# q of batches 0 and 1 loaded and transposed in the layout of k: 2 KB pieces, 64 transposes of a quarter of the array each

## The chip, the cores and the metric

The kernel runs on one core of a Trainium2 chip. The metric is the device time of one execution in microseconds; lower is better. A profiled execution also gives a *span*, from the first to the last recorded event, which is about 1.8 us shorter than the time.

## The reference, cut to what matters

A linear attention (softmax of q along its 64 features, softmax of k along its 576 tokens, no softmax of their product) is followed by a two-layer network with an exact gelu:

```python
# q, k, v: 8 batches x 8 heads x 576 tokens x 64, float32
q_s = softmax(q, axis=-1)
k_s = softmax(k, axis=2)
kv  = einsum('bhsd,bhse->bhde', k_s, v)
x   = einsum('bhsd,bhde->bhse', q_s, kv)     # -> 4608 x 512
h   = x @ w_in                               # 512 x 2048
out = gelu(h) @ w_out                        # 2048 x 512
```

The two products of the network are nearly all of the work. They run in bfloat16 as matmuls of 128x128 weights with 512 columns.

## The kernel before: the parts that matter

Tokens are worked off in nine groups of 512. Eight groups hold 512 of a batch's 576 tokens each; the 64 that are left of every batch make up the ninth. For the attention product of a group, q must lie with its 64 features along the partitions. Batches 0 and 1, which are needed early, are transposed by TensorE; the others by a DMA. Before, a partition held four consecutive tokens of every head, so one piece of memory was 4 x 64 x 4 B = 1 KB:

```python
def load_main(b, name, t, parts=1):          # q of batches 0 and 1, in two transfers
    ...
    src = t[b, :, 0:M, :].rearrange("h (p j) d -> p h (j d)", j=J)      # M = 512, J = 4
    ...

def exp_q(b, parts=1):
    ...
    if parts == 1:      # four instructions of 512 columns, each touching heads of both halves
        sets = [(slice(i, None, 4), slice(u, None, 4)) for i, u in ((0, 0), (1, 1), (2, 3), (3, 2))]
    else:               # six instructions; the first three complete heads 0 to 3
        sets = []
        for h in (0, 4):
            sets += [(slice(h + i, h + i + n), slice(h + u, h + u + n))
                     for i, u, n in ((0, 0, 2), (2, 3, 1), (3, 2, 1))]
    for i, u in sets:
        nc.scalar.activation(out=dst[:, i], in_=src[:, u], func=AF.Exp)

def tp_mm(b, half):                          # 8 transposes of 128x128: two heads x 64 features
    ...
    for i in range(2):
        hp = 2 * half + i
        for j in range(J):
            nc.tensor.transpose(ps[:, j, i, :],
                st[b]["eq"][:, j, 2 * hp:2 * hp + 2, :].rearrange("p h d -> p (h d)"), identity)
```

A word on names, for the profiles below. L355 is line 355 of that kernel's file, so the same operation has another number in each kernel. `e` and `ek` are exp of q and of k, `qsum` the sums by which q is normalised, `qT` the transposed q, `kvc` the normalised product of k and v, `ps` and `tp` banks of the accumulator memory, `xT` the result of the attention product and the input of the first big product, `g` the gelu's output, `wi_bf` and `wo_bf` the two weights. A *tile* of the first big product is 128 of its 2048 columns and takes four matmuls of 0.216 us.

The normalising of q is done in halves (four heads each), the first half on GpSimd and the second on VectorE. Batch 2 is the first whose q is transposed by a DMA. That transfer sits in the second product of batch 1, and the attention product of batch 2 (`x_all(2)`) follows later in the same stage:

```python
exp_q(2, parts=2)
exp_k(2)
exp_k(3)
exp_q(3)
table(AF.Gelu)
y_phase(1, {
    (0, 15): [lambda: norm_q(2, 0, 2)],
    (1, 1): [lambda: norm_q(2, 1, 2, nc.vector)],
    (1, 14): [lambda: kv_step(2)],
    (1, 15): [lambda: xbar_step(2)],          # q of batch 2 transposed by a DMA
    (2, 2): [lambda: cast_v_all(3), lambda: load(4)],
    (3, 5): [lambda: x_all(2), lambda: kv_step(3)],
})
```

The softmax here doesn't subtract the row's maximum and nothing guards it: scores larger than these inputs give would overflow.

## Time and profile before

| | kernel before |
|---|---|
| time, three executions ahead of the prediction | 279.63 to 279.91 us |
| span of the profile | 278.0 us |
| TensorE busy | 270.0 us |
| first matmul of the first big product | 14.32 us |
| second big product of batch 0 begins | 28.15 us |
| attention product of batch 2 begins | 70.98 us |

The last rows are stations on TensorE's road. TensorE is the bound, so a change matters by what it does to the time at which TensorE comes past such a station. What TensorE itself waited for is a short list. Its columns are: who waits, for whom, us in total, how often, and the longest; "issue" is time in which the engine waited for nothing that the profile shows.

```profile
PE ps L475 <- DVE zeros L500: 1.5, 1, 1.5
PE ps L355 <- issue: 1.1, 7, 0.2
PE ps L294 <- DVE kvc L218: 0.6, 1, 0.6
PE kv L199 <- ACT v_aug L160: 0.2, 1, 0.2
```

The first is the warming at the very start. The other two named waits are short and lie in batch 0's start. No wait on a transfer appears: in particular none on the transposed q of batch 2.

### The profile page before, as it was taken

The page shows a single profiled execution, that of the slowest core. Times are in us where ns is not written, and L with a number is a line of the kernel's source. Part 1 is how long each engine was busy: PE and PEld are TensorE (multiplying, and loading weights), DVE is VectorE, ACT ScalarE, POOL GpSimd, SP SyncE. Part 2 cuts the span into 40 slices and gives each one's busy share as a digit, 9 for nine tenths or more (in the row PEclk, how much of TensorE's full clock was granted, in tenths as well). Part 3 has the DMA queues.
Part 4 walks back from the last instruction along what each step waited for, and adds up shares of the span by engine and source line. Part 5 has one row for each costly group of instructions (what it writes and reads, how often), then busy time and mean ns, then how long its engine had stood idle before and what let it go on. Part 6 is the DMA issues. An engine that isn't in the chain of part 4 may idle for free.

```text
span 278.0 us, 4534 instructions
## 1 busy us (share of the span) xinstructions
PE 270.0 (97%) x1891; PEld 126.5 (46%) x1919; DVE 100.7 (36%) x153; ACT 158.0 (57%) x247; POOL 32.8 (12%) x26
## 2 busy tenths in 40 slices
PE   7899999999999999999999999999999999999995
PEld 3444454444444444444444444444444444444443
DVE  2876574319743540093008400651015200130012
ACT  4867675789377816791569246943683363136400
POOL 1520051002020220014000500050005000000000
PEclk9999999999999999999999999999999999999999
DMA  7999999963993139702981199017502500220033
GB/s 253 398 386 429 397 402 407 398 257 103 287 348 61 66 79 295 283 38 86 267 329 40 42 247 383 38 51 190 115 0 75 151 2 0 75 78 0 0 78 77
DMA packets 44980, 50.10 MB, mean 180 GB/s; under 512 B 20384, under 2 KB 29856, under 8 KB 44704
## 3 DMA queue, kind: packets, MB, share of 16 engines
q1 hardware_dynamic: 44560, 49.39, 53.5%
q10 hardware_dynamic: 400, 0.43, 0.6%
q8 instruction: 15, 0.25, 0.3%
q14 instruction: 5, 0.04, 0.0%
HBM read 36.70 MB, written 9.44 MB: 166 GB/s over the span
## 4 chain that ended last, share of the span: by engine, by line
PE 94%; DMA 2%; issue 1%; ACT 1%; SPq 1%; DVE 0%
PE ps L327 44%; PE ps L355 43%; DMA f<-in_k_dram 2%; PE kv L199 2%; PE ps L294 2%; PE ps L380 1%; PE pair L327 1%; ACT ek L150 0%; ACT v_aug L160 0%; PE ps L255 0%; SPq L90 0%; PE ps L299 0%; SPq L103 0%; PE tp L255 0%; DVE kvc L218 0%
## 5 line engine op out<-in xcount | busy, mean ns | idle before, releaser
L327 PE MATMUL ps<-xT,wi_bf 128*128 128x512 bf16 x557 | 124.2, 380 | 0.5
L355 PE MATMUL ps<-wo_bf,g 128*128 128x512 bf16 x543 | 122.1, 380 | 1.6 <-issue 1.1
L333 ACT ACTIVATE g<-ps 128x512 bf16<-128x512 f32 x142 | 83.5, 598 | 66.8 <-PE ps L327 66.8
L327 PEld LDWEIGHTS <-wi_bf 128*128 128x128 bf16 x576 | 56.1, 98 | 68.0 <-issue 0.5
L355 PEld LDWEIGHTS <-g 128*128 128x128 bf16 x560 | 53.9, 98 | 64.3 <-issue 0.4
L363 DVE COPY y_sb<-ps 128x512 f32<-128x512 f32 x33 | 22.7, 687 | 81.7 <-PE ps L355 78.6
L238 POOL TENSOR_TENSOR e<-e,recq 128x2048 bf16<-128x2048 bf16 (+1 forms) x9 | 25.7, 2855 | 176.2 <-DVE recq L237 141.5
L162 DVE CAST v_aug<-f 128x576 bf16<-128x576 f32 x24 | 16.4, 746 | 47.5 <-DMA f<-in_v_dram 47.5
L236 DVE TENSOR_REDUCE qsum<-e 128x16 f32<-128x1024 bf16 (+1 forms) x13 | 21.1, 1621 | 14.4 <-ACT e L145 14.3
L320 ACT CAST xT<-ps 128x512 bf16<-128x512 f32 x18 | 9.9, 588 | 28.8 <-PE ps L294 18.8
L145 ACT ACTIVATE e<-f 128x512 bf16<-128x512 f32 (+1 forms) x42 | 20.5, 556 | 3.5 <-DMA f<-in_q_dram 3.5
L150 ACT ACTIVATE ek<-f 128x2304 bf16<-128x2304 f32 (+1 forms) x10 | 17.2, 1728 | 0.5 <-DMA f<-in_k_dram 0.4
L318 DVE CAST xT<-ps 128x512 bf16<-128x512 f32 x17 | 11.0, 686 | 17.0 <-PE ps L294 14.1
L79 ACT ACT_TABLE_LOAD x9 | 11.5, 1283 | 2.8 <-issue 2.6
L475 PE MATMUL ps<-zeros 128*128 128x512 f32 (+1 forms) x15 | 9.2, 773 | 1.5 <-DVE zeros L500 1.5
L145 ACT ACT_TABLE_LOAD x7 | 9.0, 1283 | 0.1
L431 DVE CAST wi_bf<-w 128x512 bf16<-128x512 f32 x12 | 7.3, 654 | 2.2 <-DMA w<-in_moe_w_in_dram 1.9
L199 PEld LDWEIGHTS <-ek 64*64 64x64 bf16 x576 | 6.6, 105 | 2.6 <-ACT wo_bf L470 0.4
L199 PE MATMUL kv<-v_aug,ek 64*64 64x65 bf16 x576 | 7.2, 194 | 0.2 <-ACT v_aug L160 0.2
L294 PE MATMUL ps<-qT,kvc 64*64 64x512 bf16 x62 | 5.7, 391 | 0.8 <-DVE kvc L218 0.6
L238 DVE TENSOR_TENSOR e<-e,recq 128x1024 bf16<-128x1024 bf16 x4 | 6.2, 1546 | 0.1
L475 PEld LDWEIGHTS ps<-zeros 128*128 128x128 f32 x14 | 3.5, 260 | 6.0 <-issue 4.5
(39 smaller groups left out, 49.9 us busy)
## 6 DMA issues: line engine op xcount, KB each, us to landing
out_dram<-y_sb SPq DMA_DIRECT2D x32, 256.0 KB, 2.4
f<-in_k_dram SPq DMA_DIRECT2D x6, 1152.0 KB, 9.7
f<-in_v_dram SPq DMA_DIRECT2D x6, 1152.0 KB, 11.7
f<-in_q_dram SPq DMA_DIRECT2D x6, 1024.0 KB, 7.2
w<-in_moe_w_in_dram SPq DMA_DIRECT2D x6, 512.0 KB, 8.7
f<-in_v_dram SPq DMA_DIRECT2D x8, 288.0 KB, 6.8
f<-in_q_dram SPq DMA_DIRECT2D x4, 512.0 KB, 12.5
w<-in_moe_w_out_dram SPq DMA_DIRECT2D x2, 1024.0 KB, 11.7
```

The costliest lines, as they stand in the source:

```text
L79: nc.scalar.activation(out=scr[:, 1:2], in_=scr[:, 0:1], func=func)
L145: nc.scalar.activation(out=dst[:, i], in_=src[:, u], func=AF.Exp)
L150: nc.scalar.activation(out=ek[b % 2][:, i:i + n], in_=st[b]["kf"][:, i:i + n].rearrange("p x (n d) -> p x n d", n=NS), func=AF.Exp,)
L162: eng.tensor_copy(out=o, in_=i)
L199: nc.tensor.matmul(st[b]["kv"][hp][c, 0:D + 1], ek[b % 2][pr, hp, n, :], v_aug[b % 2][pr, hp, n, 0:D + 1], start=(n == 0), stop=(n == NS - 1),
L236: nc.vector.reduce_sum(out=qsum, in_=eq[:, :, hs, :], axis=AX.X)
L238: eng.tensor_tensor(out=eq[:, :, hs, :], in0=eq[:, :, hs, :], in1=recq.unsqueeze(3).to_broadcast([128, J, w, D]), op=ALU.mult,)
L327: nc.tensor.matmul(ps, wi_bf[:, dm, t * 128:(t + 1) * 128], st[c]["xT"][:, dm, :], start=(dm == 0), stop=(dm == NDM - 1),)
L333: nc.scalar.activation(out=st[c]["g"][:, t, :], in_=ps, func=AF.Gelu)
L355: nc.tensor.matmul(ps, st[c]["g"][:, t, j * 128:(j + 1) * 128], wo_bf[:, t, :], start=(t == 0), stop=(t == NDF - 1),)
L363: nc.vector.tensor_copy(out=y_sb, in_=ps)
L475: nc.tensor.matmul(ps, z[:, 0:128], z, start=True, stop=True)
```

## The change

It fetches q of batches 0 and 1 as k is fetched: a partition belongs to one of the two heads of a pair and holds eight of every nine consecutive tokens, one piece of 8 x 64 x 4 B = 2 KB. Each head's transpose is then 64x64, and four of them can stand in the quadrants of the array at once. The second product of batch 0's attention moves in between the first matmuls of the big product. Outputs of batches 0 and 1 are written in two transfers of 64 rows each. The branch with two parts in `exp_q` is deleted: `exp_q(2, parts=2)` becomes `exp_q(2)`. The core of the diff, cut:

```diff
+    def load_qpair(b):
+        f = f32in.tile([128, HP, M], FP32, tag="qf", name="f")
+        src = q[b].rearrange("h (p n) d -> (h p) (n d)", n=NS).rearrange("(x q) f -> q x f", q=128)
+        for i in (0, 2):
+            nc.sync.dma_start(out=f[:, i:i + 2, :], in_=src[:, i:i + 2, 0:M])
 ...
+    def tpq_mm(b, half):
+        for n in range(NQ):                                   # NQ = 8
+            for i in range(2):
+                for hh in range(2):
+                    hp = 2 * half + i
+                    pr = slice(hh * 64, hh * 64 + 64)
+                    c = slice((hh ^ i) * 64, (hh ^ i) * 64 + 64)
+                    nc.tensor.transpose(st[b]["tp"][hp][c, n, :], st[b]["eq"][pr, hp, n, :],
+                                        identity[pr, pr])
 ...
-    def exp_q(b, parts=1):
+    def exp_q(b):
-        if parts == 1:
-            sets = [...four...]
-        else:
-            sets = [...six, half by half...]
+        sets = [...four...]
 ...
+            for i in range(2):                                # outputs of batches 0 and 1
+                nc.sync.dma_start(out=dst[2 * j + i], in_=y_sb[i * 64:i * 64 + 64, :])
 ...
     kv_norm(0, 1)
-    x_evac(0, 1)
+    for t in range(2):
+        h_mm(0, hps[t], t, (0,))                              # two big matmuls, then
     x_tile(0, 3, psum_h, "h")
     x_mm(0, 1)                                                # the second attention product
 ...
-    exp_q(2, parts=2)
+    exp_q(2)
```

More of the change, by code (lines that the diff above doesn't have):

```diff
@@ L44 @@
     NS = S // 64
+    NQ = M // 64
     VW = D + 2
@@ L90, in load_main @@
             nc.sync.dma_start(out=f[:, i * n:(i + 1) * n, :], in_=src[:, i * n:(i + 1) * n, :])
+    def load_qpair(b):
+        f = f32in.tile([128, HP, M], FP32, tag="qf", name="f")
+        st[b]["qf"] = f
+        src = q[b].rearrange("h (p n) d -> (h p) (n d)", n=NS).rearrange("(x q) f -> q x f", q=128)
+        for i in (0, 2):
+            nc.sync.dma_start(out=f[:, i:i + 2, :], in_=src[:, i:i + 2, 0:M])
     def load_pair(b, name, t, parts=1):
@@ L115, in load, with rest @@
         load_pair(b, "v", v)
+    def rest(b):
+        return slice(NQ, S, NS) if b < 2 else slice(M, S)
     def load_qrest():
@@ L123, in load_qrest, with exp_qpair @@
                 out=f[(b % 2) * R:(b % 2 + 1) * R, b // 2, :, :],
-                in_=q[b, :, M:S, :].rearrange("h p d -> p h d"),
+                in_=q[b, :, rest(b), :].rearrange("h p d -> p h d"),
             )
-    def exp_q(b, parts=1):
+    def exp_qpair(b):
+        e = attn_sb.tile([128, HP, NQ, D], BF16, tag="eq", name="e")
+        st[b]["eq"] = e
+        for i in range(2):
+            nc.scalar.activation(
+                out=e[:, 2 * i:2 * i + 2],
+                in_=st[b]["qf"][:, 2 * i:2 * i + 2].rearrange("p x (n d) -> p x n d", n=NQ),
+                func=AF.Exp,
+            )
@@ new lines, in norm_qpair, with tpq_tiles, bank @@
+    def norm_qpair(b, i, eng):
+        eq = st[b]["eq"][:, 2 * i:2 * i + 2].rearrange("p x n d -> p (x n) d")
+        qsum = small.tile([128, 2 * NQ], FP32, tag="qsum", name="qsum")
+        recq = small.tile([128, 2 * NQ], FP32, tag="recq", name="recq")
+        nc.vector.reduce_sum(out=qsum, in_=eq, axis=AX.X)
+        nc.vector.reciprocal(recq, qsum)
+        eng.tensor_tensor(
+            out=eq, in0=eq, in1=recq.unsqueeze(2).to_broadcast([128, 2 * NQ, D]), op=ALU.mult,
+        )
+    def tpq_tiles(b):
+        def bank(pool, tag):
+            return pool.tile([128, 2, NQ, 64], BF16, tag=tag, name="tp")[:, 0]
+        if b == 0:
+            st[b]["tp"] = [bank(psum_y, "y"), bank(psum_y, "y"), bank(psum_a, "a"), bank(psum_h, "h")]
+        else:
+            ps = psum_a.tile([128, 2, 2, NQ, 64], BF16, tag="a2", name="tp")
+            st[b]["tp"] = [bank(psum_a, "a"), bank(psum_h, "h"), ps[:, 0, 0], ps[:, 1, 0]]
+            st[b]["tp2"] = ps[:, :, 0]
@@ new lines, in tpq_mm @@
+    def tpq_mm(b, half):
+        if half == 0:
+            st[b]["qT"] = attn_sb.tile([128, HP, NQ, 64], BF16, tag="qT", name="qT")
+        for n in range(NQ):
[4 more added lines that the diff above has]
+                    c = slice((hh ^ i) * 64, (hh ^ i) * 64 + 64)
+                    nc.tensor.transpose(
+                        st[b]["tp"][hp][c, n, :], st[b]["eq"][pr, hp, n, :], identity[pr, pr],
+                    )
@@ L129, in exp_q, with tpq_evac @@
+    def tpq_evac(b, hp, eng="v"):
+        if hp == "last":
+            nc.vector.tensor_copy(out=st[b]["qT"][:, 2:4], in_=st[b]["tp2"])
+            return
+        o, i = st[b]["qT"][:, hp], st[b]["tp"][hp]
+        if eng == "v":
+            nc.vector.tensor_copy(out=o, in_=i)
+        else:
+            nc.scalar.copy(out=o, in_=i)
+    def exp_q(b):
         e = attn_sb.tile([128, J, H, D], BF16, tag="eq")
@@ L136, in exp_q @@
             src = src.rearrange("p h (j d) -> p h j d", j=J)
-        if parts == 1:
-            sets = [(slice(i, None, 4), slice(u, None, 4)) for i, u in ((0, 0), (1, 1), (2, 3), (3, 2))]
-        else:
-            sets = []
-            for h in (0, 4):
-                sets += [(slice(h + i, h + i + n), slice(h + u, h + u + n))
-                         for i, u, n in ((0, 0, 2), (2, 3, 1), (3, 2, 1))]
+        sets = [(slice(i, None, 4), slice(u, None, 4)) for i, u in ((0, 0), (1, 1), (2, 3), (3, 2))]
         for i, u in sets:
@@ L166, in cast_v_all, with kv_tiles @@
             cast_v(b, hp)
-    def kv_tiles(b):
-        if b == 0:
+    def kv_tiles(b, half):
+        if b == 0 and half == 1:
             p = [psum_h.tile([128, 512], FP32, tag="h", name="kv")[:, 0:256] for i in range(2)]
-            ps = psum_a.tile([128, 4, 256], FP32, tag="a2", name="kv")
-            st[b]["kvall"] = ps[:, 0::2]
-            p += [ps[:, 0, :], ps[:, 2, :]]
-        else:
+            st[b]["kv"] += p
+        elif "kv" not in st[b]:
             ps = psum_a.tile([128, 4, 256], FP32, tag="a2", name="kv")
             st[b]["kvall"] = ps
-            p = [ps[:, i, :] for i in place]
-        st[b]["kv"] = p
+            st[b]["kv"] = [ps[:, 0, :], ps[:, 2, :]] if b == 0 else [ps[:, i, :] for i in place]
     place = [1, 2, 0, 3]
@@ L188, in kv_mm @@
     def kv_mm(b, half):
-        if "kv" not in st[b]:
-            kv_tiles(b)
+        kv_tiles(b, half)
         for n in range(NS):
@@ L208, in kv_norm @@
             parts = [(ps, kvc[b], 4)]
-        elif b == 0 and half == 0:
-            parts = [(st[b]["kv"][hp].unsqueeze(1), kvc[b][:, hp:hp + 1], 1) for hp in range(2)]
+        elif b == 0 and half == 1:
+            parts = [(st[b]["kv"][hp].unsqueeze(1), kvc[b][:, hp:hp + 1], 1) for hp in (2, 3)]
         elif b == 0:
-            parts = [(ps, kvc[b][:, 2:4], 2)]
+            parts = [(ps[:, 0::2], kvc[b][:, 0:2], 2)]
         else:
@@ L241, in norm_q @@
         )
-    def tp_mm(b, half):
-        if half == 0:
-            st[b]["qT"] = attn_sb.tile([128, J, HP, 128], BF16, tag="qT", name="qT")
-        if b == 1 and half == 1:
-            ps = psum_a.tile([128, 2, J, 2, 128], BF16, tag="a2", name="tp")[:, 0]
-        else:
-            pool, tag = (psum_h, "h") if half == 1 else (psum_a, "a")
-            ps = pool.tile([128, J, 2, 128], BF16, tag=tag)
-        st[b][f"tp{half}"] = ps
-        for i in range(2):
-            hp = 2 * half + i
-            for j in range(J):
-                nc.tensor.transpose(
-                    ps[:, j, i, :],
-                    st[b]["eq"][:, j, 2 * hp:2 * hp + 2, :].rearrange("p h d -> p (h d)"),
-                    identity,
-                )
-    def tp_evac(b, half, eng="v"):
-        o = st[b]["qT"][:, :, 2 * half:2 * half + 2, :]
-        if eng == "v":
-            nc.vector.tensor_copy(out=o, in_=st[b][f"tp{half}"])
-        else:
-            nc.scalar.copy(out=o, in_=st[b][f"tp{half}"])
-    def tp_step(b, half):
-        tp_mm(b, half)
-        tp_evac(b, half)
     def xbar_step(b):
@@ L293, in x_mm @@
                     if b < B:
+                        qT = st[b]["qT"][pr, hp] if b < 2 else st[b]["qT"][pr, :, hp]
                         nc.tensor.matmul(
-                            ps[c, :], kvc_of(b, hp)[pr], st[b]["qT"][pr, :, hp, :],
-                            start=True, stop=True,
+                            ps[c, :], kvc_of(b, hp)[pr], qT, start=True, stop=True,
                         )
@@ L365, in y_out @@
             nc.scalar.copy(out=y_sb, in_=ps)
-        if c < B:
+        if c < 2:
+            dst = out[c * S:(c + 1) * S, :].rearrange("(p n) f -> n p f", n=NS)
+            for i in range(2):
+                nc.sync.dma_start(out=dst[2 * j + i], in_=y_sb[i * 64:i * 64 + 64, :])
+        elif c < B:
             dst = out[c * S:c * S + M, :].rearrange("(p j) n -> p j n", j=J)[:, j, :]
@@ L370, in y_out @@
             for b2 in range(2):
-                r0 = (2 * j + b2) * S + M
-                nc.sync.dma_start(out=out[r0:r0 + R, :], in_=y_sb[b2 * R:(b2 + 1) * R, :])
+                b = 2 * j + b2
+                nc.sync.dma_start(
+                    out=out[b * S:(b + 1) * S, :][rest(b)], in_=y_sb[b2 * R:(b2 + 1) * R, :]
+                )
     def y_last():
@@ L438, in cast_wi_dm @@
         w = w[:, dm, 0:n].rearrange("p (m c) -> p c m", c=r)
-        if eng is nc.scalar:
-            eng.copy(out=o, in_=w)
-        else:
-            eng.tensor_copy(out=o, in_=w)
+        eng.tensor_copy(out=o, in_=w)
     def load_wo(i):
@@ L475, in warm @@
             nc.tensor.matmul(ps, z[:, 0:128], z, start=True, stop=True)
-    load_main(0, "q", q, 2)
+    load_qpair(0)
     load_pair(0, "k", k, 2)
@@ L489 @@
     wo = [load_wo(i) for i in range(3)]
-    load_main(1, "q", q, 2)
+    load_qpair(1)
     load_pair(1, "k", k, 2)
@@ L506 @@
     table(AF.Exp)
-    exp_q(0, parts=2)
+    exp_qpair(0)
     exp_k(0, parts=2)
-    norm_q(0, 0, 2)
-    norm_q(0, 1, 2, nc.vector)
-    tp_mm(0, 0)
+    norm_qpair(0, 0, nc.gpsimd)
+    norm_qpair(0, 1, nc.vector)
+    tpq_tiles(0)
+    tpq_mm(0, 0)
     cast_v(0, 0, nc.scalar)
     cast_v(0, 1, nc.scalar)
-    tp_evac(0, 0, "s")
-    warm(1)
+    tpq_evac(0, 0, "s")
+    tpq_evac(0, 1, "s")
     cast_v(0, 2, nc.gpsimd)
@@ L519 @@
     x_tile(0, 1, psum_y, "y")
+    x_tile(0, 2, psum_a, "a")
     kv_mm(0, 0)
     kv_norm(0, 0)
-    tp_mm(0, 1)
-    tp_evac(0, 1)
-    x_tile(0, 2, psum_a, "a")
+    tpq_mm(0, 1)
+    tpq_evac(0, 2)
+    tpq_evac(0, 3)
     x_mm(0, 0)
     x_evac(0, 0, "s")
-    cast_wi_dm(0, wi[0], 0, nc.scalar)
-    for dm in range(1, NDM):
+    x_evac(0, 1, "s")
+    for dm in range(NDM):
         cast_wi_dm(0, wi[0], dm, nc.gpsimd)
@@ L531 @@
     kv_norm(0, 1)
-    x_evac(0, 1)
+    h_begin(0)
+    ps = psum_a.tile([128, 2, M], FP32, tag="a2", name="ps")
+    hps = [ps[:, t] for t in range(2)]
+    for t in range(2):
+        h_mm(0, hps[t], t, (0,))
     x_tile(0, 3, psum_h, "h")
     x_mm(0, 1)
-    x_evac(0, 2, "s")
-    x_evac(0, 3)
+    x_evac(0, 2)
+    x_evac(0, 3, "s")
     cast_wi(1, wi[1], "p")
     table(AF.Gelu)
+    for dm in (1, 2, 3):
+        for t in range(2):
+            h_mm(0, hps[t], t, (dm,))
+    for t in range(2):
+        h_gelu(0, hps[t], t)
+    cast_wi(2, wi[2], "v")
     def ybank():
@@ L550 @@
     h_phase(0, {
-        0: [lambda: cast_wi(2, wi[2], "v")],
         2: [lambda: cast_wi(3, wi[3], "v")],
@@ L555 @@
         12: [lambda: cast_wo(1, wo[1])],
-    }, groups={0: 2, 4: 4, 8: 4}, banks={
+    }, t1=2, groups={4: 4, 8: 4}, banks={
         3: ybank, 6: ybank, 8: ybank,
@@ L560 @@
     })
-    exp_q(1, parts=2)
+    exp_qpair(1)
     exp_k(1, parts=2)
@@ L566 @@
     cast_wo(2, wo[2])
+    tpq_tiles(1)
     yps = [psum_h.tile([128, DM], FP32, tag="h", name="ps") for j in range(2)]
     yps += [psum_y.tile([128, DM], FP32, tag="y", name="ps") for j in range(2)]
-    norm_q(1, 0, 2)
-    norm_q(1, 1, 2, nc.vector)
+    norm_qpair(1, 0, nc.gpsimd)
+    norm_qpair(1, 1, nc.vector)
     cast_wo(3, wo[3], 0, 2)
@@ L580 @@
         y_part(t, range(J))
-    tp_step(1, 0)
-    tp_step(1, 1)
+    tpq_mm(1, 0)
+    tpq_evac(1, 0)
+    tpq_evac(1, 1)
+    tpq_mm(1, 1)
+    tpq_evac(1, "last")
     load(3)
```

## The prediction

> **What bounds the kernel now.** I read the page first (shares of the engines, the chain that ended last), then the chain in order of time, then the timeline of three stretches: the start, the middle of batch 0's second product, and the first transfer that transposes. The times are 279.63 to 279.91 us and the profiled span is 278.0 us, so 1.9 us lie outside the span.
>
> ```profile
> PE 270.0 (97%) x1891; PEld 126.5 (46%) x1919; DVE 100.7 (36%) x153; ACT 158.0 (57%) x247; POOL 32.8 (12%) x26
> ...
> PE 94%; DMA 2%; issue 1%; ACT 1%; SPq 1%; DVE 0%
> PE ps L327 44%; PE ps L355 43%; DMA f<-in_k_dram 2%; PE kv L199 2%; PE ps L294 2%; PE ps L380 1%; PE pair L327 1%; ACT ek L150 0%; ACT v_aug L160 0%; PE ps L255 0%; SPq L90 0%; PE ps L299 0%; SPq L103 0%; PE tp L255 0%; DVE kvc L218 0%
> ```
>
> The chain is TensorE for 94%. The two big products (L327, L355) are 1152 full columns' worth of 512-wide matmuls, untouched by the change. A later batch's first product runs from 103.44 to 117.25 us in the chain, 64 matmuls in 13.81 us, 0.216 each; 1152 of them are 248.6 us. So the change can win only in what is left: the start before the stream (14.3 us), small work put into the stream, and waits in it. The chain in order of time shows the start:
>
> ```profile
> 2.34 6.62 DMA f<-in_k_dram
> ...
> 8.98 1.16 ACT ek L150
> 10.15 1.15 ACT v_aug L160 x2
> 11.33 0.47 PE kv L199 x34
> ...
> 13.64 0.30 DVE kvc L218
> 13.98 0.41 PE ps L294 x4
> 14.39 0.75 PE ps L327 x3
> ```
>
> Read it downwards: the second half of k lands at 8.96 us, and everything after is a string of short steps up to the first L327. exp of q is not in it. The timeline adds what the chain does not: the first weights come late too.
>
> ```profile
> 13.31 1.12 POOL L442 CAST wi_bf<-w 128x256 bf16<-128x256 f32 x3 [0.75 <-DMA w<-in_moe_w_in_dram]
> 13.58 0.42 ACT L440 CAST wi_bf<-w 128x256 bf16<-128x256 f32 x1
> ```
>
> GpSimd sat idle 0.75 us for them and got them at about 13.3 us.
>
> **What the Trainium skill says.** "TensorEngine Tiling (Array Packing)", Key Properties: changing the tiling mode drains TensorE. The trace agrees: before the quadrant product at 43.03 us the last full-width matmul started about 42.72 (its end, 43.10, less 0.38), 0.31 us earlier, where full-width ones follow at 0.216; so a change of mode costs about 0.1 us. "ScalarE: Activation LUTs", What ACT_TABLE_LOAD costs: an ACTIVATE takes 186 ns plus 0.833 ns per element, and neighbours overlap by about 93 ns. The trace agrees: 1.16 us at 1152 elements, and four of 512 in 2.17 us. "DMA: Bandwidth & Descriptors", Specifications: 512 B is the least transfer for line rate. Pieces of 1 KB and of 2 KB would then be alike; the trace agrees only roughly: 362 to 366 GB/s from 3 to 5 us, mostly q in 1 KB pieces, 401 to 410 from 7 to 11 us, k and v in 2304 B pieces, but 387 to 397 when the first weights, also 1 KB, move.
>
> **The change part by part.**
>
> (a) *The load and exp of q.* Two 2 KB pieces per partition and transfer in place of four of 1 KB. 1.05 MB at 364 GB/s are 2.88 us and at 400 would be 2.62; at the weights' 1 KB rate of 392, 2.67. I take 0.15 us, between 0.05 and 0.26, for k, v and the weights behind q too. exp becomes two instructions of 1024 for three (512, 256, 256), about 1.04 for 1.24 us, twice. That is beside the wait for k: worth nothing itself.
>
> (b) *Batch 0 up to the stream.* Shifting the chain by 0.15: k at 8.81, exp of k to 9.99, both casts of v to 11.15, first kv product to 11.65. ScalarE then does two evacuations of 128x512 instead of one of 128x1024 (estimate from the 512-wide casts: 0.59 each, 0.52 apart): 11.2 to 12.3. The first x product starts there, about 12.25, ends 12.7. xT of pair 0 is out at 13.35. Normalising kv (0.17 + 0.29) and two vector evacuations (1024 bf16 took 0.68, f32 512 took 0.69, hence 0.42 for 512 bf16) fill VectorE from 11.7 to 13.05; then the two separate norms (0.75 as at 11.84 to 12.59) end at 13.8.
>
> Now the new order bites. Two L327 matmuls stand ahead of the second x product. They need the first weights: landed at about 13.15, cast by GpSimd in 0.38 a slice, so at 13.55. They start at 13.57 and 13.79; x follows after the drain at 14.1, not at 13.87 when its kvc is ready. Its evacuation (0.69) ends at 15.25. By then two more L327 matmuls are done, and the other four of tiles 0 and 1 start there: tile 2 starts at 15.27 + 4 x 0.216 = 16.13. Before, the first L327 starts at 14.32 and runs on without a gap, so tile 2 starts at 14.32 + 8 x 0.216 = 16.05. **Part (b) gives -0.1 us, with 0.2 either way.** It is a rearrangement: four matmuls go early, but the last xT comes no sooner.
>
> (c) *Batch 1's transposes, in the stream.* Before:
>
> ```profile
> 38.67 0.45 PE ps L255 x8
> 39.12 0.45 PE tp L255 x8
> ...
> 65.27 0.71 PE kv L199 x72
> 65.98 0.16 issue
> ```
>
> 16 transposes of 128x128 cost 0.90 us. The change makes 64 of 64x64, in four quadrants as kv's matmuls are: 72 of these cost 0.71 + 0.16, so 64 cost about 0.63 + 0.16 plus a drain, 0.85 to 0.95. **Nothing won, 0.05 lost.** Their evacuations (0.42, 0.42, 0.68 on VectorE) end about 40.7; the next user of the bank, kv at 41.3, doesn't wait.
>
> (d) *exp of batch 2.* This side effect I hold for the largest. `parts=2` goes: exp of q for batch 2 no longer finishes one half of the heads first. The timeline:
>
> ```profile
> 60.52 2.37 ACT L145 ACTIVATE e<-f 128x512 bf16<-128x512 f32 x6
> 61.80 1.22 DVE L236 TENSOR_REDUCE qsum<-e 128x16 f32<-128x1024 bf16 x1 [8.64 <-ACT e L145]
> ...
> 65.29 1.23 DVE L238 TENSOR_TENSOR e<-e,recq 128x1024 bf16<-128x1024 bf16 x1
> ...
> 66.68 1.69 SPq L274 DMA_TRANSPOSE qT<-e  x1
> 66.83 2.17 ACT L145 ACTIVATE e<-f 128x512 bf16<-128x512 f32 x4
> ...
> 70.98 0.63 PE L294 MATMUL ps<-qT,kvc 64*64 64x512 bf16 x8
> ```
>
> The first sum started 1.28 after exp, once three of six were done. Now it needs all four of 512, which take 2.17 (last but one line): start 2.21 after exp, 0.93 later. VectorE is back to back from there to the second half's scaling at 66.52, so the transposing transfer is issued 0.93 later. It took 3.8 us to land (DMA issues of that stretch), 70.48; the x product started at 70.98. Slack 0.5, less some 0.05 for the semaphore. **The new wait is 0.93 - 0.45 = 0.48 us,** in the stream, on the path.
>
> (e) *The rest.* Outputs of batches 0 and 1 go in two transfers of 64 rows instead of one of 128: eight more issues on SyncE, at 0.3 to 0.5 us each, while the outputs are not waited for. The order of the built program shows that every issue waits for the one eight earlier; the transposing one's is an output transfer long done. 0. The warming matmul that goes ran at 10.60 in idle time: 0.
>
> Sum: 0.1 + 0.05 + 0.48 = 0.6 us more; I take off some of it, because (b) would turn to a gain if q comes 0.25 earlier: 279.9 + 0.4 = **280.3 us**.
>
> **The rivals.** *The start wins.* If the whole start is bound by the transfers, and 2 KB pieces gain 0.26 or more, tile 2 starts 0.1 to 0.3 earlier, and with quadrant transposes at 0.6 without a drain the sum is 0.5 won before 60 us. Batch 2's wait then takes about as much back, since exp of batch 2 moves along with the stream: 279.7 to 279.9. For it speak the 364 against 406 GB/s; against it the first weights' 387 to 397 at the same 1 KB. *Quadrant transposes do not run side by side.* If 64 of them took 0.056 each as 128x128 ones do, batch 1 would lose 3.6 - 0.9 = 2.7 us, and the start some more: 283 us or over. Against it speak kv's matmuls of the same shape, 10 ns each. *ScalarE becomes the bound of batch 0.* Gelu cannot start before the table load (1.28) behind the last evacuation: about 16.6, for 16.44 now. The fourth of the next group waits for tile 2's gelu, about 18.2, and TensorE comes there at 18.5: hidden by 0.3; it caps what the start could win. *Batch 2's transfer lands sooner than 3.8 us*: then (d) shrinks and the time is the old one.
>
> **Range and chances.** The parts' uncertainties are 0.2 in (b), 0.15 in (c), 0.2 in (d), and a run's own 0.3: 279.5 to 281.1 us. A change of 2% is 5.6 us; neither the 14.3 us of the start nor anything added is apt to move by that: faster 0.01, same 0.98, slower 0.01.
>
> **What would show it right or wrong.** (a) exp of k's second half at 8.7 to 8.9, not 8.98. (b) The first L327 near 13.6, then a gap until the last xT near 15.2, and tile 2 near 16.1. (c) The 64 transposes of batch 1 within 0.95 us. (d) The first sum of batch 2 about 2.2 us after its exp begins, and a TensorE wait of 0.3 to 0.7 us on the transposed qT ahead of that x product, where none is now. Most apt to be wrong: the size of (a), and in (b) when the weights land; if TensorE has no wait near 71 us, the sum is wrong by 0.5.

## The result, and the profile after

| | before | after |
|---|---|---|
| time, median of 6 executions each | 279.63 us (279.60 to 279.91) | 280.31 us (280.21 to 280.80) |
| ratio, 95% interval | | 1.0025 (1.0012 to 1.0038) |
| span of the profiled execution | 278.0 us | 278.8 us |

Ratios in this document are the mean time of one kernel's runs over that of the other's of the same rounds, so not quite the ratio of the medians quoted beside them. The change costs 0.7 us of 280. The profiled execution was the slowest of the six (280.80); the other five had spans of 278.3 to 278.5, so the profile shows some 0.4 us that is not typical. Read it together with the repeat below.

The page of the kernel after; the first line has busy time, share and instructions of each engine, the others the chain that ended last:

```profile
PE 269.4 (97%) x1986; PEld 125.4 (45%) x2014; DVE 99.8 (36%) x154; ACT 157.4 (56%) x238; POOL 33.0 (12%) x27
...
PE 72%; DMA 22%; DVE 2%; issue 1%; ACT 1%; SPq 1%; ACTq 0%
```

TensorE has less work (269.4 for 270.0 us), and yet the span is longer. The chain now runs through transfers for 22%. This share misleads: followed back from one late landing, the chain slides onto the transfers that came before it. The waits of TensorE in the same profile say how much it really waited for each (left out: the warming's 1.5, 1.1 of "issue", and 0.2 on qsum, which takes the place of one "issue"):

```profile
PE ps L360 <- POOL wi_bf L478: 0.7, 1, 0.7
PE kv L261 <- ACT v_aug L226: 0.5, 1, 0.5
PE ps L328 <- DMA qT<-e: 0.4, 1, 0.4
PE ps L328 <- DVE kvc L280: 0.3, 1, 0.3
PE ps L360 <- DVE xT L351: 0.3, 1, 0.3
```

Four of the five lie in batch 0's start, where they replace others. The third is new and stands in the middle of the stream: the attention product of batch 2 waits for the transfer that transposes its q.

**The start.** The timeline of the kernel after (start, us, engine, line, operation, count, and in brackets the idle time ahead of it and what ended it):

```profile
13.16 1.48 POOL L478 CAST wi_bf<-w 128x256 bf16<-128x256 f32 x4 [0.73 <-DMA w<-in_moe_w_in_dram]
...
13.63 0.39 PE L360 MATMUL ps<-xT,wi_bf 128*128 128x512 bf16 x1 [0.67 <-POOL wi_bf L478]
14.17 0.41 PE L328 MATMUL ps<-qT,kvc 64*64 64x512 bf16 x4
14.51 0.61 PE L360 MATMUL ps<-xT,wi_bf 128*128 128x512 bf16 x2
14.62 0.69 DVE L351 CAST xT<-ps 128x512 bf16<-128x512 f32 x1 [0.86 <-PE ps L328]
...
15.37 2.97 PE L360 MATMUL ps<-xT,wi_bf 128*128 128x512 bf16 x13 [0.25 <-DVE xT L351]
```

The big product starts 0.69 us earlier than before (13.63 for 14.32), stops, and goes on at 15.37 when the last xT is there. At 16.05 the old order was past its first eight matmuls; the new one is at 15.37 + 4 x 0.216 = 16.23.

**Batch 1's transposes.** TensorE's timeline of the kernel before, then after:

```profile
28.15 10.52 PE L355 MATMUL ps<-wo_bf,g 128*128 128x512 bf16 x47
38.51 0.61 PE L255 MATMUL ps<-identity,e 128*128 128x128 bf16 x8
38.95 0.61 PE L255 MATMUL tp<-identity,e 128*128 128x128 bf16 x8
39.40 1.89 PE L355 MATMUL ps<-wo_bf,g 128*128 128x512 bf16 x8
```

```profile
28.64 10.52 PE L388 MATMUL ps<-wo_bf,g 128*128 128x512 bf16 x47
39.09 0.74 PE L185 MATMUL tp<-identity,e 64*64 64x64 bf16 x64
39.76 1.90 PE L388 MATMUL ps<-wo_bf,g 128*128 128x512 bf16 x7
```

From start to start, the 16 transposes took 39.40 - 38.51 = 0.89 us and the 64 take 39.76 - 39.09 = 0.67. Getting into the other mode costs 0.09 (28.64 to 39.09 is 10.45, 28.15 to 38.51 is 10.36). The stretch from the stage's start to the resumed product is 11.12 us for 11.25: 0.13 won.

**Batch 2's q.** TensorE's timeline of the kernel before (the rest of this stretch of it stands in the prediction, part (d)), then that of the kernel after, all engines, picked out:

```profile
66.14 4.91 PE L355 MATMUL ps<-wo_bf,g 128*128 128x512 bf16 x22 [0.16 <-issue]
70.98 0.63 PE L294 MATMUL ps<-qT,kvc 64*64 64x512 bf16 x8
```

```profile
60.89 2.19 ACT L211 ACTIVATE e<-f 128x512 bf16<-128x512 f32 x4
...
63.11 1.22 DVE L298 TENSOR_REDUCE qsum<-e 128x16 f32<-128x1024 bf16 x1 [9.01 <-ACT e L211]
...
66.50 4.91 PE L388 MATMUL ps<-wo_bf,g 128*128 128x512 bf16 x22 [0.16 <-DVE qsum L298]
66.61 1.23 DVE L300 TENSOR_TENSOR e<-e,recq 128x1024 bf16<-128x1024 bf16 x1
...
67.97 1.74 SPq L307 DMA_TRANSPOSE qT<-e  x1
...
71.79 0.63 PE L328 MATMUL ps<-qT,kvc 64*64 64x512 bf16 x8 [0.38 <-DMA qT<-e]
```

The first sum starts 2.22 us after exp begins, where it was 1.28 before. The transposing transfer is issued at 67.97 for 66.68 and takes 3.77 us to land (the chain's figure); TensorE stands for it 0.38 us. From the 22 matmuls ahead to the attention product it is 5.29 us for 4.84 (66.14 to 70.98 before).

These three pieces add up to the whole difference of the two profiles: 0.49 at the start (28.64 - 28.15), -0.13 at the transposes, 0.45 at batch 2, sum 0.81; the spans differ by 0.8. Between the stations the two kernels take the same time: 39.40 to 66.14 and 39.76 to 66.50 are both 26.74 us.

### The profile page after: what moved, and what is told of

Read it like the earlier page. It is cut to its first block, busy times and chain, and to the rows that moved or that the text cites. A ratio compares the mean times of both kernels' runs of the same rounds, so it can differ in the third digit from the quotient of the medians.

```text
span 278.8 us, 4729 instructions
## 1 busy us (share of the span) xinstructions
PE 269.4 (97%) x1986; PEld 125.4 (45%) x2014; DVE 99.8 (36%) x154; ACT 157.4 (56%) x238; POOL 33.0 (12%) x27
## 4 chain that ended last, share of the span: by engine, by line
PE 72%; DMA 22%; DVE 2%; issue 1%; ACT 1%; SPq 1%; ACTq 0%
PE ps L360 35%; PE ps L388 34%; DMA w<-in_moe_w_out_dram 7%; DMA f<-in_q_dram 5%; DMA w<-in_moe_w_in_dram 3%; DMA out_dram<-y_sb 2%; DMA f<-in_k_dram 2%; DMA qT<-e 1%; PE ps L419 1%; PE ps L328 1%; PE kv L261 1%; DVE qsum L298 1%; DVE wi_bf L470 1%; ACT e L211 1%; DVE e L300 0%
## 5 line engine op out<-in xcount | busy, mean ns | idle before, releaser
L300 POOL TENSOR_TENSOR e<-e,recq 128x2048 bf16<-128x2048 bf16 (+1 forms) x7 | 21.9, 3128 | 150.1 <-DVE recq L299 122.5
L298 DVE TENSOR_REDUCE qsum<-e 128x32 f32<-128x2048 bf16 (+1 forms) x9 | 16.2, 1801 | 9.0 <-ACT e L211 9.0
L351 DVE CAST xT<-ps 128x512 bf16<-128x512 f32 x16 | 10.4, 686 | 17.3 <-PE ps L328 14.4
L211 ACT ACTIVATE e<-f 128x512 bf16<-128x512 f32 x28 | 15.3, 616 | 0.1
L511 PE MATMUL ps<-zeros 128*128 128x512 f32 x14 | 8.6, 783 | 1.5 <-DVE zeros L536 1.5
L159 POOL TENSOR_TENSOR e<-e,recq 128x1024 bf16<-128x1024 bf16 x2 | 3.8, 1900 | 26.7 <-DVE recq L158 26.7
L157 DVE TENSOR_REDUCE qsum<-e 128x16 f32<-128x1024 bf16 x4 | 4.8, 1205 | 5.3 <-ACT e L146 5.3
L146 ACT ACTIVATE e<-f 128x1024 bf16<-128x1024 f32 x4 | 4.2, 1056 | 4.1 <-DMA f<-in_q_dram 4.1
```

Source lines behind the costliest of these rows:

```text
L298: nc.vector.reduce_sum(out=qsum, in_=eq[:, :, hs, :], axis=AX.X)
L300: eng.tensor_tensor(out=eq[:, :, hs, :], in0=eq[:, :, hs, :], in1=recq.unsqueeze(3).to_broadcast([128, J, w, D]), op=ALU.mult,)
L351: nc.vector.tensor_copy(out=st[b]["xT"][:, hp, :], in_=ps)
```

## The experiments

**Theory.** The loss that repeats is batch 2's: deleting the six-piece exp makes its sums, the transfer behind them and the attention product late. Start and transposes nearly cancel. **Rivals.** (R1) The start, with its new order and its late weights, is the loss. (R2) The split outputs delay the transposing transfer, which SyncE issues behind them. (R3) Batch 2's transfer is fixed in time, so that whatever is won at the start is waited away there. A further question, of time beyond the span, came up in the runs and is the last experiment. All kernels were run beside the kernel before, on one chip in each series.

### The changed kernel once more

No edit; the file is run again, beside the next three.

> The changed kernel once more, as the control of this series: 0.6 to 0.75 us above the kernel before (ratio 1.0022 to 1.0027). Its first profile had a dip in the transfer rate near 14 us (115 to 152 GB/s for three quarter-microseconds, where the kernel before fell to 229 to 283) and was the slowest of six runs (280.8 against 280.21 to 280.53). If the dip belongs to that run alone, this profile's span is 278.2 to 278.5 us and the last matmul of batch 0's first product ends about 0.2 us later than in the kernel before, not 0.5. If the dip belongs to the change, it is there again and the delay is 0.5 again.

Measured: 280.87 us (279.93 to 281.86, 6 runs) for 279.60 (279.44 to 279.97, 11 runs); ratio 1.0046 (1.0027 to 1.0065). That is more than the 0.6 to 0.75 expected: 1.27 by the medians, though the median span rose by 0.5 only (278.3 for 277.8). TensorE's timeline:

```profile
66.02 4.91 PE L388 MATMUL ps<-wo_bf,g 128*128 128x512 bf16 x22 [0.16 <-DVE qsum L298]
71.26 0.63 PE L328 MATMUL ps<-qT,kvc 64*64 64x512 bf16 x8 [0.33 <-DMA qT<-e]
```

The second big product starts at 28.15, exactly as before, where the first profile had 28.64; the transposes win 0.13 again (39.27); the attention product of batch 2 starts at 71.26 for 70.98. So the 0.49 at the start belongs to one execution, and batch 2's loss stays (5.24 us for 4.84). Five spans were 278.2 to 278.4 and one 280.1, but times scattered more than spans: time less span was 1.73 to 3.20 us. That spread was not expected.

### The changed kernel with exp of batch 2 in halves again

```diff
-    def exp_q(b):
+    def exp_q(b, parts=1):      # with the six-piece branch back
 ...
-    exp_q(2)
+    exp_q(2, parts=2)
```

> The changed kernel, but exp of q of batch 2 again in the kernel before's six pieces, half of the heads first. Theory: the wait of 0.4 us on the transposed qT near 71 us comes from this part alone; it goes (first sum 1.28 us after exp begins, not 2.2), and the time falls by 0.4 to 0.45 us against the changed kernel, to about 0.25 us above the kernel before. Rival (the late part of the time is lost to the outputs' split transfers or to DMA, and the wait is only where it shows): the wait stays or another takes its place, and the time stays within 0.1 us of the changed kernel.

Measured: 279.60 us (279.55 to 279.62, 5 runs), ratio to the kernel before 0.9999 (0.9986 to 1.0012). TensorE's timeline:

```profile
66.02 4.91 PE L394 MATMUL ps<-wo_bf,g 128*128 128x512 bf16 x22 [0.16 <-issue]
70.86 0.63 PE L334 MATMUL ps<-qT,kvc 64*64 64x512 bf16 x8
```

The stretch is 4.84 us again and the wait is gone, with the new load, order, transposes and split outputs all still in. This one call therefore carries the loss within the span, and R2 falls: the outputs are still split and nothing waits. Two more runs of this kernel followed.

> The changed kernel with exp of batch 2 in halves, again, beside the kernel with 1 KB pieces on the same chip: the time of before within 0.15 us; span 277.8.

Measured: 279.78 us (279.50 to 279.96, 4 runs), ratio 0.9996 (0.9981 to 1.0011). The second big product started at 28.49 in this profile: the start scatters by 0.3 us with nothing changed.

> The partner of the run above: exp of batch 2 in halves, the early matmuls ahead of x as in the change. The time of before within 0.1 us.

Measured: 279.77 us (279.50 to 280.92, 6 runs), ratio 1.0014 (0.9999 to 1.0030), start at 28.17. Four runs were 279.50 to 279.78; two were at 280.77 and 280.92 with ordinary spans (277.9, 278.1).

### The kernel before with exp of batch 2 in quarters

```diff
-    exp_q(2, parts=2)
+    exp_q(2)
```

> The kernel before with this one part of the change alone: exp of q of batch 2 in four pieces. Theory: a wait of 0.4 to 0.5 us on the transposed qT appears ahead of batch 2's x product and the time rises by 0.4 to 0.5 us. Rival as for the run before: no change beyond 0.1 us.

Measured: 280.19 us (280.05 to 280.51, 5 runs), ratio 1.0022 (1.0010 to 1.0034). VectorE's and TensorE's timeline:

```profile
62.63 1.22 DVE L236 TENSOR_REDUCE qsum<-e 128x16 f32<-128x1024 bf16 x1 [8.98 <-ACT e L145]
...
66.02 4.91 PE L355 MATMUL ps<-wo_bf,g 128*128 128x512 bf16 x22 [0.16 <-DVE qsum L236]
71.30 0.63 PE L294 MATMUL ps<-qT,kvc 64*64 64x512 bf16 x8 [0.37 <-DMA qT<-e]
```

exp begins at 60.41 here, so the first sum is again 2.22 us behind it. One line, in the old kernel, brings the same wait. It costs 0.59 us, all of it within the span (median 278.4 for 277.8), as much as the changed kernel beside it lost there (278.3). What the changed kernel lost besides, up to its 1.27 us in these rounds, lies beyond the span and is not this line's: here the time less span was 1.75 to 1.81. Undone in the new kernel and done in the old one, the line does the same. R1 is not needed for it.

### Batch 1 alone

The kernel before, with load, exp, normalising, transposes and split outputs of batch 1 as in the changed kernel; batches 0 and 2 stay.

```diff
-    load_main(1, "q", q, 2)
+    load_qpair(1)
 ...
-    exp_q(1, parts=2)
+    exp_qpair(1)
 ...
-    tp_step(1, 0)
-    tp_step(1, 1)
+    tpq_mm(1, 0)
+    tpq_evac(1, 0)
+    tpq_evac(1, 1)
+    tpq_mm(1, 1)
+    tpq_evac(1, "last")
```

> The kernel before with q of batch 1 alone loaded and transposed in the new way (64 quadrant transposes in the stream), batch 0, its order, and exp of batch 2 as before. What the two profiles show: 64 quadrant transposes held the stream for 0.67 us (39.09 to 39.76) where 16 full ones held it 0.89 (38.51 to 39.40). Theory: this part alone wins 0.2 us (0.1 to 0.3), ratio about 0.9993. Rival, as in the prediction: nothing won or 0.05 lost, and the 0.22 was an accident of two single traces.

Measured: 279.71 us (279.63 to 280.10, 5 runs), ratio 1.0007 (0.9995 to 1.0018). In the trace the stretch is 28.13 to 39.25, 11.12 us: the 0.13 is there as in every kernel with these transposes. The time does not show it, and the interval reaches from 0.14 us won to 0.5 lost. Unresolved at this size.

### The attention product ahead of the two early matmuls

In the changed kernel, and in the one with the halves back, the second attention product of batch 0 was moved to the front again:

```diff
-    for t in range(2):
-        h_mm(0, hps[t], t, (0,))
     x_tile(0, 3, psum_h, "h")
     x_mm(0, 1)
+    for t in range(2):
+        h_mm(0, hps[t], t, (0,))
```

> The changed kernel with the x product ahead of the two early matmuls alone; exp of batch 2 stays in quarters. Theory: what is won in batch 0 (0.2 to 0.3 us) moves exp of batch 2 too, so it isn't swallowed by the wait near 71 us, which stays 0.3 to 0.4 us: about 0.25 us below the changed kernel, spans near 278.05. Rival: the wait on the transposed qT is tied to something fixed in time (a transfer's turn), grows by what was won, and the time stays.

Measured, in the changed kernel: 280.03 us (279.91 to 280.36, 4 runs), ratio 1.0019 (1.0005 to 1.0034). The second big product starts at 27.93, the earliest so far, and TensorE still waits at batch 2, at an earlier hour:

```profile
65.80 4.91 PE L388 MATMUL ps<-wo_bf,g 128*128 128x512 bf16 x22 [0.16 <-DVE qsum L298]
71.04 0.63 PE L328 MATMUL ps<-qT,kvc 64*64 64x512 bf16 x8 [0.33 <-DMA qT<-e]
```

R3 falls: 5.24 us, as in the repeat of the changed kernel, though the stage came 0.22 us earlier. The wait moves along with the stream, since exp of batch 2 starts behind the last gelu before it and one table load (58.28 + 0.60, then 1.28, and exp at 60.19).

> The changed kernel with exp of batch 2 in halves again (as the run that came back to the time of before), and in batch 0 the second x product ahead of the two early matmuls of the first big product. Theory: the early matmuls wait for the first weights (cast ended 13.43 in that run) and hold x back, which could start when its kvc is ready, about 13.65, but started at 14.01; with x first, its last xT is out 0.3 us earlier, tile 2 of the first product starts at 15.75 to 15.85 for 16.07, and the time falls by 0.2 to 0.3 us, to about 279.35, ratio to before 0.9990 to 0.9994. Rival: the next weights (512 columns further on) land no sooner, in a dip of the transfer rate near 14 us, and hold the stream a little later: nothing is won, the second big product starts at 28.1 again, 279.6.

Measured, with the halves back: 279.77 us (279.53 to 281.23, 6 runs), ratio 1.0014 (0.9999 to 1.0030). TensorE's timeline:

```profile
13.48 0.74 PE L334 MATMUL ps<-qT,kvc 64*64 64x512 bf16 x4 [0.53 <-DVE kvc L286]
14.16 4.06 PE L366 MATMUL ps<-xT,wi_bf 128*128 128x512 bf16 x17
```

The gap of the changed kernel's start has gone: the big product starts at 14.16 and runs on. The stage after starts at 27.98 for 28.16, and five of six spans were 277.7 to 277.9. The times do not show 0.2 us.

> The candidate for the best version, again, beside the one without x first on one chip: exp of batch 2 in halves and x ahead of the early matmuls. Theory: 0.1 to 0.25 us below the run beside it and below the kernel before (ratio to before about 0.9994), as its first trace had the second big product at 27.98 and not at 28.16. Rival: the start varies by as much from run to run, and the two cannot be told apart: within 0.1 us.

Measured: 279.58 us (279.40 to 280.72, 5 runs), ratio 0.9999 (0.9986 to 1.0012); start at 27.95. The profiled execution is the one of 280.72, and TensorE was not the reason: VectorE's last copy began at 274.29, ahead of the 274.61 of the kernel before, and the span is still 278.9, because the last outputs took longer to land: 3.7 us for 2.4 on ScalarE's queue, 3.3 for 2.0 on SyncE's. The median span is 277.6 for 277.9, so an order that wins some 0.2 us within the span is likely; the times do not confirm it. No version was found that beats the kernel before by more than the scatter.

### The dose: a whole exp of k ahead of exp of q

```diff
-    exp_q(2)
     exp_k(2)
+    exp_q(2)
```

> A dose test of the wait near 71 us: the changed kernel with exp of k of batch 2 ahead of its exp of q, which puts q's exp 2.06 us later (one 2304-wide exp took 2.06 us on ScalarE) and changes nothing else of batch 2's chain. Theory (exp, sums, scaling and the transposing transfer are one chain whose slack is used up): the wait of 0.3 to 0.4 us on the transposed qT grows by about 2.06 us, less what kv of batch 2 then no longer overlaps, to 2.2 to 2.6 us, and the time to about 282.2 to 282.6. Rival (the wait is set by the transfer's turn in its queue, behind the outputs): the wait grows by much less than 2 us, and the time stays below 281.

Measured: 282.15 us (281.99 to 283.06, 4 runs), ratio 1.0089 (1.0069 to 1.0109). ScalarE's and TensorE's timeline:

```profile
60.62 2.12 ACT L216 ACTIVATE ek<-f 128x2304 bf16<-128x2304 f32 x1
62.65 2.17 ACT L211 ACTIVATE e<-f 128x512 bf16<-128x512 f32 x4
...
66.96 3.61 PE L388 MATMUL ps<-wo_bf,g 128*128 128x512 bf16 x16 [0.89 <-DVE y_sb L396]
70.77 1.46 PE L388 MATMUL ps<-wo_bf,g 128*128 128x512 bf16 x6 [0.20 <-DVE y_sb L396]
73.50 0.63 PE L328 MATMUL ps<-qT,kvc 64*64 64x512 bf16 x8 [1.27 <-DMA qT<-e]
```

exp of q is 2.03 us later (62.65 - 60.62), and the attention product comes 45.14 us after the stage of batch 0's second product began (28.36), for 43.11 in the repeat of the changed kernel (28.15 to 71.26): 2.03 later. The dose goes through in full. It is spread over two waits: 1.27 on the transfer (0.33 in the repeat, and 2.2 to 2.6 expected), and 1.09 on output copies that VectorE could do only after its late sums. The second was not foreseen.

### 1 KB pieces with the new layout

The kernel with the halves back, with batch 0's q fetched in column halves, so that pieces are 1 KB again, in four transfers:

```diff
-            nc.sync.dma_start(out=f[:, i:i + 2, :], in_=src[:, i:i + 2, 0:M])
+            for c in ((0, M // 2), (M // 2, M)) if b == 0 else ((0, M),):
+                nc.sync.dma_start(out=f[:, i:i + 2, c[0]:c[1]], in_=src[:, i:i + 2, c[0]:c[1]])
```

> The changed kernel with exp of batch 2 in halves, and batch 0's q in the new layout, but fetched in pieces of 1 KB again (four transfers for two). It tells whether the size of the pieces makes k and the weights land earlier. Theory: k's second exp starts 0.2 to 0.4 us later than with 2 KB pieces (8.6 becomes 8.85 to 9.0), the first weights at 13.2 to 13.35 for 13.0, the second big product at 28.3 to 28.5 for 28.16, the time 0.1 to 0.3 us higher; the dip of the transfer rate near 14 us (0.45 to 0.67 us lost against 400 GB/s in five traces with the new load, 0.26 to 0.33 in three with the old) shrinks to about 0.3. Rival (it is not the size of the pieces but which rows are read together): nothing moves by 0.1.

Measured: 283.52 us (282.94 to 284.87, 4 runs), ratio 1.0137 (1.0110 to 1.0164). Most of this is not the size of the pieces. SyncE's timeline:

```profile
0.73 2.00 SPq L102 DMA_DIRECT2D f<-in_q_dram  x4
4.25 0.82 SPq L115 DMA_DIRECT2D f<-in_k_dram  x2
```

With two more transfers of q ahead, k became SyncE's fifth; elsewhere the fifth is v. In the kernels before and after and in this one the fifth is issued at 3.90, 4.26 and 4.25 us, after a wait of 1.1 to 1.5 us on a piece of k. This is the program's own wait, not a limit of the chip: ScalarE issues four transfers too, so SyncE's fifth is the ninth in all, and every issue waits for the one eight earlier (the prediction's part (e)). That one is ScalarE's first, a piece of k of 288 KB, issued at 0.74 and 3.1 to 3.5 us in landing. So k came late, TensorE had nothing from 10.65 to 12.25 us, and its clock fell. Busy time of each engine, then clock, DMA share and GB/s, in stretches of the same kernel:

```profile
11.00:12.00 1.00, 0.00 (x0) 0.00 (x0) 0.22 (x1) 1.00 (x2) 0.00 (x0) 1.00 1.02 357
12.00:12.25 0.25, 0.00 (x1) 0.00 (x0) 0.00 (x0) 0.21 (x2) 0.00 (x0) 0.90 1.09 407
...
18.00:19.00 1.00, 1.00 (x4) 0.38 (x3) 1.00 (x3) 1.00 (x1) 0.00 (x0) 0.50 1.04 391
19.00:20.00 1.00, 1.00 (x6) 0.41 (x5) 1.00 (x2) 0.80 (x3) 0.00 (x0) 0.99 1.06 412
```

The granted clock was 0.50 until 19 us. The experiment is confounded and decides nothing on the time. The rates while mostly q moves fit the idea that larger pieces go faster, and no more than that:

| GB/s | 3 to 4 us | 4 to 5 us | 5 to 6 us |
|---|---|---|---|
| before, 1 KB pieces | 366 | 362 | 383 |
| new layout, 1 KB pieces | 333 | 352 | 383 |
| after, 2 KB pieces | 399 | 385 | 408 |
| after with halves back, 2 KB pieces | 401 | 402 | 388 |

### More TensorE instructions, and nothing else

Up to here, 40 executions of the kernel before had a time less span of 1.73 to 1.87 us. Of 50 executions of kernels with batch 0's change, 18 were above 1.9. The traces point to TensorE's program. They count the transfers that fetch instructions, 16 KB each. In the kernel before (3813 TensorE instructions in the program) the last falls between 264 and 268 us. In the changed kernel (4003) it comes later or is not recorded: in the repeat, a fetch lies between 279 and 280 us, behind the span's end of 278.2; in the first profile none is seen after 248 us. In the execution of 280.72 told of above, whose last outputs landed late, it lies between 275 and 276. To separate the number of instructions from all else, the kernel before got 96 small matmuls of zeros at its start:

```diff
+    def warm_quarters(n):        # 64x64 matmuls of zeros, four to a turn, in two banks
 ...
-    warm(7, zeros32)
+    warm(6, zeros32)
+    warm_quarters(24)
```

> The kernel before with 96 small matmuls of zeros (64x64 quadrants) put at the start in place of one of the warming matmuls: 4005 TensorE instructions for 3813, as many as the changed kernel has (4003), and nothing else of the change. What it tells apart: time beyond the profiled span. In 40 executions of the kernel before, run time less span was 1.73 to 1.87 us; in 50 executions of kernels with the change of batch 0, 18 were above 1.9 (up to 3.2), and one more had its last output land a microsecond late within the span. Theory: TensorE's instruction stream is fetched in pieces of 16 KB, and with 190 more instructions one further fetch falls due near 273 us, when the program is ending (seen at 273 to 280 us, or not within the record, in the traces of the changed kernels; the last one of the kernel before falls at 264 to 268); it then holds up the end in some executions. It expects here the fetch at 244 to 248 us, then one at 273 us or later or beyond the record, and about a third of the executions over 1.9 us beyond the span (or a span longer by more than 0.5 than the others); median within 0.3 of the kernel before. Rival: the lost time comes of the new load of q or of the outputs in two transfers; then all executions stay within 1.73 to 1.87 as those of the kernel before, whatever the fetches do.

Measured: 280.23 us (280.08 to 281.01, 5 runs), ratio 1.0019 (1.0005 to 1.0033). The transfers of its trace between 280 and 281 us hold one fetch (transfers, MB, share of 16 engines):

```profile
q8 instruction: 1, 0.02, 5.8%
```

Time less span was 1.73, 1.78, 1.88, 2.06 and 2.61 us; the nine runs of the kernel before beside them had 1.74 to 1.82. Old load, old outputs, and yet two of five above 1.9, where none of 49 executions of the kernel before was: the rival falls, and the number of instructions is enough. The 14 profiled executions, one of each run, sort the same way by where the last fetch of their own trace lies. Inside the span (seven, four of them with batch 0's change): time less span 1.74 to 1.82. Behind the span's end (three: this one, the repeat, and the changed kernel with the attention product ahead): 2.61, 2.34 and 1.91. Not recorded (four, all with batch 0's change): 1.82 to 2.01. How the late fetch holds up the end is argued, not shown. The share says that one of the 16 DMA engines was held for 0.058 x 16 = 0.93 us.

A part of the expectation failed: the median was to lie within 0.3 us, and it is 0.5 higher. Spans grew too (278.1 to 278.5 for 277.7 to 278.2). In this trace another fetch has moved into 13 to 14 us, and the second batch of weights came late there: GpSimd waited 1.29 us for it, for 0.23 before, and the second big product started at 28.61 for 28.15. That the fetch made them late is likely and not tested.

## Why the prediction was right

The time came out at 280.31 us against 280.3, inside the range, and "within 2%" holds. The parts were not all as told:

| step | predicted | measured |
|---|---|---|
| (a) q comes earlier | 0.15 us | k's second exp 0.40 earlier (8.58 for 8.98), kv's run 0.28 (11.05 for 11.33), weights 0.15 (13.16 for 13.31) |
| (b) order of the start | 0.1 us lost | in the profile tile 2 at 16.23 for 16.05; in the repeat 16.06 |
| (c) batch 1's transposes | 0.05 us lost | 0.13 won in every trace with them |
| (d) batch 2's exp | 0.48 us lost | 0.40 to 0.45 lost in TensorE's timeline |
| (e) split outputs, fewer warming matmuls | 0 | 0 in waits of TensorE |
| beyond the span | not considered | about 0.2 lost here, more in the repeat |

**(a)** was right in kind and too small. k's second exp began at 7.54 + 2.20 - 1.16 = 8.58 us. As foretold, what was gained shrinks on the way to the weights. The wait went over to v: TensorE waits 0.5 us for its cast.

**(b)** was right in mechanism, and in size within its 0.2 either way (0.18 lost in the profile, 0.01 in the repeat). The foretold times of the two early matmuls, of the attention product and of the four behind it were 13.57, 14.1 and 15.27; the profile has 13.63, 14.17 and 15.37. The further 0.31 us that this profile lost by 28.64 was outside the step: behind a dip of the transfer rate near 14 us weights came late (VectorE's first cast of them 16.12 for 15.32; 15.59 in the repeat, where the half microsecond from 14 us had 156 GB/s for 133 here); that the dip is the reason was not tested. From tile 2 to the second product it took 12.41 us there, 12.09 in the repeat and 12.10 before. The two experiments that restore the old order agree that it is no worse: the stage after starts about 0.2 us earlier with it (27.93 for 28.15, 27.98 for 28.16, and 27.95 in the second run of the latter; six traces with the new order have 28.15 to 28.64). So what (a) won at the start, (b) gave back.

**(c)** is the term that failed, in its sign. The prediction added a pause of 0.16 us that stands behind kv's matmuls in the trace, and a drain. The transposes took 0.67 us with everything behind them, so there was no such pause; the drain ahead of them cost 0.09. The estimate from kv's matmuls was good for the work and wrong to carry kv's pause over. The rival of quadrants that do not run side by side (2.7 us lost) is refuted by the same figure.

**(d)** was the step that mattered. The first sum came 2.22 us after exp for a foretold 2.21, the transfer landed in 3.77 for 3.8, and the wait of 0.38 lies in the foretold 0.3 to 0.7. The two experiments on that one line show cause and size from both sides. It was no part of the change's intent.

**The sum.** The median span rose from 277.9 (40 executions) to 278.4 (12), 0.5 us. The prediction's terms, with what the repeat shows, give 0 - 0.13 + 0.40 = 0.3; the rest is no more than the start scatters. The time rose by 0.7. The missing 0.2 is time beyond the span (1.81 to 2.03 us in the six executions after, where 1.8 is usual).

That 280.3 met 280.31 so closely is luck, twice over. A gain in (c) that the prediction did not have, and a cost at the program's end that it did not have either, went in opposite directions. And the forecast was a rise of 0.4 us on a base of 279.9, the middle of the three executions seen ahead; the base measured beside the change was 279.63, and the rise 0.68. The sum of the parts as first worked out, 0.63, was nearer to that than the 0.4 left after some was taken off. (The 1.9 us that the prediction puts outside the span is from this base too; the profiled execution itself took 279.74 us, 1.74 above its span.)

The rival "the start wins" is refuted by the run with the halves back: with batch 2's loss undone the new start and transposes together gain nothing that the times show.

## What to carry to other kernels

When a helper loses a branch, look at every caller: here the one call outside the intended change cost more, within the span, than all that the change itself did. The order in which an engine finishes the parts of a tile is worth keeping if a transfer stands behind the first part, even if more instructions are needed for it. And count instructions as well as their time: 190 more, nearly free on TensorE, moved an instruction fetch to the program's end, and with it went time beyond the span, which no wait in a profile of the engines shows.

## What the Trainium skill lacked or had wrong

- "DMA: Bandwidth & Descriptors", Specifications, names 512 B as enough for the full rate, while q came at 362 to 383 GB/s in pieces of 1 KB (before) and at 385 to 408 in pieces of 2 KB (after); the test meant to settle it was confounded, so it is a difference seen, not a cause shown.
- "TensorE: Matmul & The Clock Gate" has no figure for transposes smaller than 128x128. Here 64 of 64x64, in the four quadrants of the array, took 0.67 us from the first to what followed, 10 ns each, drain at the end included; 16 of 128x128 took 0.89 us, 56 ns each.
- The same page, Part 1, has the clock fall after an idle window of about 3.4 us. In the run with 1 KB pieces it fell to 0.50 at 12.2 us, after about 1.5 us without a matmul; in the 3.4 us before, TensorE had been busy for about 1.3 us (0.2 from 8.8 to 9, 0.66 from 9 to 10, and 0.45 of transposes from 10 to 11). It stayed low for 6.8 us.
- "Runtime: NRT & Kernel Launch" has no figure for an instruction fetch that falls due as the program ends. Here the time beyond the span was 1.91 to 2.61 us in the three traces that show a fetch behind the span's end, where 1.8 is usual. That the fetch is what holds up the end is not shown.
- No page tells of the dip near 14 us, when the rate fell to 133 GB/s (after) and 256 (before) for half a microsecond; with the instructions of the last experiment it did not come (371). Its cause is open.
